# Row- and column-tiled attention with separate sums for all blocks, and a rearranged start, in a fused attention and gated feed-forward kernel

## The chip, the cores and the metric

The kernel runs on one core of one Trainium2 chip. The metric is the device time of one execution in microseconds (us). Runs of one kernel that lie more than 1.5% above its fastest are called slow and are left out of the ratios. The kernel before takes 248.42 us (median of three runs, 247.49 to 248.69).

## The reference, cut to what matters

```python
# q, k, v: (4, 8, 768, 64); mem_k, mem_v: (4, 8, 8, 64); fp32
for c in range(nc):                        # chunks of 32 tokens
    k_full = concat([mem_k, k[c_start-16 : c_end+8]])   # 8 memory rows, then a band of up to 56
    v_full = concat([mem_v, v[same rows]])
    scores = q_c @ k_full.T / sqrt(64)
    a = exp(scores - max); a = a / (sum(a) + 1e-9)
    out[c] = a @ v_full
x = out, as (3072 tokens, 512)
y = (relu(x @ w_gate) * (x @ w_val)) @ w_out          # 512 -> 1536 -> 512
```

## The kernel before: the parts that matter here

The kernel works on eight blocks of 384 tokens. Each block has attention for four pairs of heads, twelve feed-forward units (a gate product and a value product, 128 columns of the inner dimension each) and three output units. The attention of block n+1 is woven between the units of block n, so that the tensor engine (PE) always has something to do. A block's attention for one pair of heads is: scores on PE, an exponential on ACT, values and sums on PE, the reciprocal of the sums on ACT (a logarithm, then an exponential of its negative), and a multiply on DVE.

For blocks 2 to 7 the kernel before loads keys and queries as rows, turns them by a DMA transpose, and lets POOL spread the queries of two heads into a block-diagonal operand, so that one 128-row product gives the scores of both. A 128-column product gives the values (64 columns) and the sums (64 columns of ones, so the sum arrives 64 times) of one head at once:

```python
X = xps.tile([128, 2, 512], F32, name="x_ps")       # one PSUM tile of two banks, used by every pair of blocks 2 to 7

def turn_dma(n):                                    # SP queue: two DMA transposes
    nc.sync.dma_start_transpose(kT, k16s[n % 2]); nc.sync.dma_start_transpose(qTs[n], q16s[n])

def spread_q(n, eng):                               # POOL, 1.46 us each, two a block
    for hh in range(2):
        s = slice(D * hh, D * hh + D)
        eng(qbds[n % 2][s, :, :, hh, :]..., qTs[n][s]...)

def step_s(n, hp):                                  # scores of a pair of heads
    for i in range(NQ):
        nc.tensor.matmul(sc[...192 columns...], lhsT=kT[:, i, hp, :], rhs=qb[:, i, hp]..., start=True, stop=True)
    # ... three exponentials on ACT

def step_v(n, hp):                                  # values and sums together; bank hh holds head hh
    for i in range(NQ):
        for hh in range(2):
            nc.tensor.matmul(X[:, hh, QB * i:QB * i + QB], lhsT=vw[:, i, 2 * hp + hh, :],
                             rhs=ex[:, i, hh, :], start=True, stop=True)
    ln = rpool.tile([D, 2, TB], F32, name="ln")
    nc.scalar.activation(ln, X[D:128, :, 0:TB], ACT.Ln, scale=1.0 / 64.0)

def step_e(n, hp):                                  # reciprocal, to SBUF
    nc.scalar.activation(rinv, lns.pop((n, hp)), ACT.Exp, scale=-1.0, bias=mln64[0:D, :])

def step_m(n, hp):                                  # two multiplies on DVE
    for hh in range(2):
        nc.vector.tensor_tensor(out=xT[D * hh:D * hh + D, hp, :], in0=X[0:D, hh, 0:TB], in1=rinv[:, hh, :], op=ALU.mult)

# ... feed-forward: g and v in two one-bank tiles of a pool of four
units[n] = [(fps.tile([128, 512], F32, tag="f", name=nm)[:, 0:TB], w, m) for m in ms for w, nm in ((wg, "g_ps"), (wv, "v_ps"))]

# ... order of the first part: attention of block 0, one unit of block 0, attention of block 1 ...
loads(2); turn_dma(2); spread_q(2, pool_copy); loads(3)     # after all weights, the output weights wo included
for m in range(2, NDC):
    ffn_unit(0, m); ffn_unit(1, m)
# ... then the six output units of blocks 0 and 1, with block 2's attention between them
```

Blocks 0 and 1 use another path: keys and queries are turned by PE, and values and sums are already split into 64-column tiles.

The softmax here doesn't subtract the row's maximum and nothing guards it: scores larger than these inputs give would overflow.

## Time and profile before

| What | Where it is read | Value |
|---|---|---|
| span of the profiled execution | page, head | 247.0 us |
| PE busy | page, part 1 | 233.5 us, 95% |
| period of one block in steady state | chain, timeline | 26.05 us |
| longest wait of PE after the start | waits | 3.3 us, for POOL's spread of block 2's queries |

The first lines are from the page: the head, PE in part 1, and the rows of PE, its granted clock and the DMA engines over 40 slices of the span, in tenths.

```profile
span 247.0 us, 4433 instructions
...
PE 233.5 (95%) x1676; PEld 135.4 (55%) x1676; DVE 99.7 (40%) x180; ACT 141.5 (57%) x269; POOL 112.6 (46%) x143
...
PE   7998989999499979999999999999999999999993
...
PEclk9999999999779999999999999999999999999998
DMA  6989999999399749997992999199711200030012
```

PE is full nearly everywhere, and from the sixteenth slice on without a gap: the kernel is bound by PE. There is one deep dent, in slice 11 (a smaller one in slice 15), and the clock is low in slices 11 and 12. The timeline of PE shows that place (columns: start, duration, engine, line, operation, operands, and in brackets the idle time before it and who ended it):

```profile
61.13 0.81 PE L331 MATMUL v_ps<-xT,wv 128*128 128x384 f16 x4
65.28 0.80 PE L253 MATMUL sc_ps<-qbd,kT 128*128 128x192 f16 x4 [3.34 <-POOL qbd L226]
65.88 5.33 PE L354 MATMUL o_ps<-wo,gv 128*128 128x512 f16 x12
```

PE waits 3.34 us for block 2's queries. Then twelve output matmuls take 5.33 us. At full clock twelve take about 2.6 us (36 take 7.77), so the half clock (granted clock 0.50 from 65 to 70 us) costs another 2.7 us. The views of the stretches show that a steady block leaves no room at all (columns: stretch, its length, then busy time and count of each engine, the granted clock, the DMA share, GB/s):

```profile
107.82:133.87 26.05, 26.05 (x181) 15.60 (x180) 11.10 (x20) 17.78 (x36) 14.54 (x16) 1.00 1.34 137
```

PE is busy 26.05 of 26.05 us. ACT is busy 17.78 and DVE 11.10. Time taken off ACT or DVE buys nothing there, and time put on PE costs all of itself, 24 pairs of heads long.

### The profile page before, as it was taken

What the parts mean: (1) busy time and instruction counts of PE and PEld (TensorE: products, weight loads), DVE (VectorE), ACT (ScalarE), POOL (GpSimd) and SP (SyncE); (2) the same over time, 40 slices, a digit from 0 to 9 for tenths busy, and PEclk for the clock granted to TensorE, in tenths of its full rate; (3) what the DMA queues carried; (4) which work ended last, traced back from release to release, by engine and by line L of the source; (5) the groups of instructions that cost most, each with busy time, mean ns of one, the idle gap of its engine ahead of it and who ended that gap; (6) DMA issues with size and microseconds to landing.
All of it is one profiled execution on the core that took longest, in us unless ns stands there. A gap on an engine that the chain in (4) does not pass through costs nothing.

```text
span 247.0 us, 4433 instructions
## 1 busy us (share of the span) xinstructions
PE 233.5 (95%) x1676; PEld 135.4 (55%) x1676; DVE 99.7 (40%) x180; ACT 141.5 (57%) x269; POOL 112.6 (46%) x143
## 2 busy tenths in 40 slices
PE   7998989999499979999999999999999999999993
PEld 2564546666245446655665466646664566556641
DVE  7666544434002134560456136521662146404410
ACT  3473763333247947872878278836884488533321
POOL 8699649960992079419905950892040000000000
PEclk9999999999779999999999999999999999999998
DMA  6989999999399749997992999199711200030012
GB/s 173 186 112 158 195 205 194 191 150 186 22 145 185 164 125 120 128 123 116 180 158 62 122 202 175 18 153 189 137 23 45 85 1 3 2 125 0 3 42 85
DMA packets 114111, 28.95 MB, mean 117 GB/s; under 512 B 101834, under 2 KB 111018, under 8 KB 114090
## 3 DMA queue, kind: packets, MB, share of 16 engines
q0 software_dynamic: 84896, 14.74, 76.7%
q1 hardware_dynamic: 28362, 13.14, 23.2%
q10 hardware_dynamic: 832, 0.79, 1.3%
q8 instruction: 13, 0.21, 0.3%
q14 instruction: 8, 0.07, 0.1%
HBM read 31.16 MB, written 6.29 MB: 152 GB/s over the span
## 4 chain that ended last, share of the span: by engine, by line
PE 71%; POOL 9%; DMA 9%; issue 7%; ACT 2%; DVE 0%; SPq 0%; POOLq 0%
PE g_ps L331 23%; PE v_ps L331 23%; PE o_ps L354 19%; DMA kst<-in_k_dram 4%; PE x_ps L273 3%; PE sc_ps L253 3%; DMA vwin<-in_v_dram 3%; POOL vwin L128 2%; POOL qbd L226 2%; DMA qT<-q16n 2%; POOL k L128 1%; POOL q16n L149 1%; POOL lq L480 1%; POOL lk L479 1%; ACT lnw L308 1%
## 5 line engine op out<-in xcount | busy, mean ns | idle before, releaser
L339 DVE TENSOR_TENSOR gv<-v_ps,gr 128x384 f16<-128x384 f32 x96 | 53.4, 557 | 97.4 <-ACT gr L338 71.4
L331 PE MATMUL g_ps<-xT,wg 128*128 128x384 f16 x384 | 80.0, 326 | 1.6 <-DVE xT L315 1.6
L331 PE MATMUL v_ps<-xT,wv 128*128 128x384 f16 x384 | 80.0, 326 | 0.2 <-ACT o_sb L357 0.2
L354 PE MATMUL o_ps<-wo,gv 128*128 128x512 f16 x288 | 66.9, 390 | 0.0
L338 ACT ACTIVATE gr<-g_ps 128x384 f16<-128x384 f32 x96 | 46.7, 487 | 31.4 <-DVE gv L339 21.8
L331 PEld LDWEIGHTS <-wv 128*128 128x128 f16 x384 | 36.4, 98 | 24.7 <-issue 2.5
L331 PEld LDWEIGHTS <-wg 128*128 128x128 f16 x384 | 37.2, 98 | 23.1 <-issue 0.4
L354 PEld LDWEIGHTS <-gv 128*128 128x128 f16 x288 | 28.6, 100 | 33.3 <-issue 2.7
L226 POOL COPY qbd<-qT 64x1536 f16<-64x1536 f16 x12 | 17.5, 1462 | 60.8 <-DMA qT<-q16n 60.4
L288 DVE TENSOR_TENSOR xT<-x_ps,rinv 64x384 f16<-64x384 f32 x48 | 26.4, 550 | 26.0 <-ACT rinv L281 25.7
L357 ACT COPY o_sb<-o_ps 128x512 f32<-128x512 f32 x24 | 14.1, 587 | 37.7 <-PE o_ps L354 37.7
L260 ACT ACTIVATE ex<-sc_ps,bias 128x256 f16<-128x256 f32 x72 | 28.6, 467 | 7.4 <-PE sc_ps L253 7.4
L128 POOL DMA_DIRECT2D vwin<-in_v_dram x32 | 29.1, 941 | 0.8 <-PE v_ps L331 0.6
L276 ACT ACTIVATE ln<-x_ps 64x768 f32<-64x768 f32 x24 | 19.4, 807 | 13.5 <-PE x_ps L273 13.4
L281 ACT ACTIVATE rinv<-ln,mln 64x768 f32<-64x768 f32 x24 | 22.2, 924 | 0.1
L128 POOL DMA_DIRECT2D k<-in_k_dram x24 | 21.5, 905 | 0.0
L149 POOL DMA_DIRECT2D q16n<-in_q_dram x24 | 18.7, 805 | 0.0
L253 PE MATMUL sc_ps<-qbd,kT 128*128 128x192 f16 x96 | 12.1, 250 | 4.3 <-POOL qbd L226 4.3
L273 PEld LDWEIGHTS <-vwin 128*128 128x128 f16 x192 | 11.1, 99 | 5.3 <-issue 1.4
L273 PE MATMUL x_ps<-ex,vwin 128*128 128x96 f16 x192 | 12.3, 207 | 1.1 <-ACT ex L260 1.1
L253 PEld LDWEIGHTS <-kT 128*128 128x128 f16 x96 | 8.7, 99 | 7.8 <-issue 4.8
L431 PE MATMUL idle<-filler 128*128 128x512 f16 x28 | 10.0, 491 | 1.3 <-DVE filler L370 1.3
(70 smaller groups left out, 104.6 us busy)
## 6 DMA issues: line engine op xcount, KB each, us to landing
out_dram<-o_sb SPq DMA_DIRECT2D x24, 256.0 KB
vwin<-in_v_dram POOLq DMA_DIRECT2D x24, 120.0 KB, 6.3
q16n<-in_q_dram POOLq DMA_DIRECT2D x24, 96.0 KB, 4.9
k<-in_k_dram POOLq DMA_DIRECT2D x18, 120.0 KB, 4.3
wo<-in_moe_w_out_dram POOLq DMA_DIRECT2D x3, 512.0 KB, 13.6
wg<-in_moe_w_gate_dram POOLq DMA_DIRECT2D x2, 512.0 KB, 9.8
wv<-in_moe_w_val_dram POOLq DMA_DIRECT2D x2, 512.0 KB, 11.6
kst<-in_k_dram SPq DMA_DIRECT2D x4, 224.0 KB
```

The lines of the kernel that those rows point to most:

```text
L128: pool_dma(dsts[p][NMEM + m0:NMEM + m1, i, :, 0:D], src)
L149: pool_dma(q16s[n][:, i], src)
L226: eng(qbds[n % 2][s, :, :, hh, :].rearrange("p i a m -> p (i a) m"), qTs[n][s].rearrange("p i a m -> p (i a) m"))
L253: nc.tensor.matmul(sc[:, i // 2, 192 * (i % 2):192 * (i % 2) + 192], lhsT=kT[:, i, hp, :], rhs=qb[:, i, hp].rearrange("p h m -> p (h m)"), ...
L260: nc.scalar.activation(dst, src, ACT.Exp, scale=SCALE, bias=bias[:, g:g + 1])
L273: nc.tensor.matmul(X[:, hh, QB * i:QB * i + QB], lhsT=vw[:, i, 2 * hp + hh, :], rhs=ex[:, i, hh, :], start=True, stop=True)
L281: nc.scalar.activation(rinv, lns.pop((n, hp)), ACT.Exp, scale=-1.0, bias=mln64[0:D, :])
L288: nc.vector.tensor_tensor(out=xT[D * hh:D * hh + D, hp, :], in0=X[0:D, hh, 0:TB], in1=rinv[:, hh, :], op=ALU.mult)
L331: nc.tensor.matmul(ps, lhsT=w[:, f, 128 * m:128 * m + 128], rhs=xTs[n][:, f, :], start=(f == 0), stop=(f == NFC - 1))
L338: nc.scalar.activation(gr, g_ps, ACT.Relu)
L339: nc.vector.tensor_tensor(out=gvs[n][:, m, :], in0=v_ps, in1=gr, op=ALU.mult)
L354: nc.tensor.matmul(o_ps, lhsT=gvs[n][:, m, 128 * t:128 * t + 128], rhs=wo[:, m, :], start=(m == 0), stop=(m == NDC - 1))
```

## The change

The change gives all blocks one way of doing attention. Scores use two 64-row tiles, so that POOL's spread and its buffers go. Sums (`step_d`) are products of their own with a small tile of ones, apart from the values (`step_v`), both in 64-column tiles, so that the reciprocal is one wide operation for both heads (128x384), its logarithm in place in PSUM. The gate and value products of a unit share one two-bank PSUM tile. Block 0's units begin earlier and run while block 1's rows load; block 2's keys and queries load before the output weights. Heads 4 to 7 of block 0 are cast by the DMA that loads them.

```diff
-    rpool = ctx.enter_context(tc.tile_pool(name="rpool", bufs=2))
+    rpool = ctx.enter_context(tc.tile_pool(name="rpool", bufs=4))
-    fps = ctx.enter_context(tc.tile_pool(name="fps", bufs=4, space=bass.MemoryType.PSUM))
+    fps = ctx.enter_context(tc.tile_pool(name="fps", bufs=2, space=bass.MemoryType.PSUM))
     X = xps.tile([128, 2, 512], F32, name="x_ps")
+    xo, xs = X[:, 0, 0:TB], X[:, 1, 0:TB]
...
-    def spread_q(n, eng): ...
+    def score_mms(n, hp, sc, start):
+        for i in range(NQ):
+            for hh in range(2):
+                s = slice(D * hh, D * hh + D)
+                nc.tensor.matmul(sc[:, hh, QB * i:QB * i + QB], lhsT=kT[s, i, hp, :], rhs=qT[s, i, hp, :], ...)
...
+    def step_d(n, hp):
+        ...     nc.tensor.matmul(xs[D * hh:D * hh + D, QB * i0:QB * i1], lhsT=ones[:, kind, :], rhs=ex[:, hh, i0:i1, :], ...)
+    def step_l(n, hp):
+        nc.scalar.activation(xs, xs, ACT.Ln, scale=1.0 / 64.0)
+    def step_e(n, hp):
+        nc.scalar.activation(rinv, xs, ACT.Exp, scale=-1.0, bias=mln64)
     def step_v(n, hp):
+        ...     nc.tensor.matmul(xo[D * hh:D * hh + D, QB * i:QB * i + QB], lhsT=vw[:, i, 2 * hp + hh, :], rhs=ex[:, hh, i, :], ...)
+    def step_m(n, hp):
+        nc.vector.tensor_tensor(out=x_of(n)[:, hp, :], in0=xo, in1=rinvs.pop((n, hp)), op=ALU.mult)
...
+        units[n] = [(fps.tile([128, 2, 512], F32, tag="f", name="f_ps"), m) for m in ms]
...
+    loads_kq(2)
     for a in range(0, NDC, 4):
         pool_dma(wo[:, a:a + 4, :], wo_src[:, a:a + 4, :])
+    turn_dma(2)
...
+    def run(order, n, first, gap, wait, turn_at):
+        ...     unit(b, x, between(n, [(w, hp) for hp in now for w in "dlv"]))
+                pieces(n, [("e", hp) for hp in now])
+    run([(1, m) for m in range(6)] + [(0, NDC + t) for t in range(NT)] + [(1, m) for m in range(6, NDC + NT)],
+        2, 6, 2, 2, 9)
     for n in range(2, NB):
+        loads(n + 2)
+        run([(n, u) for u in range(NDC + NT)], n + 1, 0, 3, 2, 9)
```

The order "dlv" is: sums, logarithm, values, and after the unit the exponential.

## The prediction

> **What bounds it now.** TensorE: busy 95% of the 247.0 us span (page, part 1). From 93 us on it is gap-free. The chain and the timeline show one block of 384 tokens every 26.05 us (107.82 to 133.87): 24 half units of 0.65, outputs 7.77, attention 2.68 (four times scores 0.33 and values 0.33). FFN and outputs of eight blocks are a floor of 187 us; attention of blocks 2 to 7 is 16; the tail after the last output matmul 3.8. The other 40 us are the target:
> - to 34.48 us (timeline, PE) the attention of blocks 0 and 1 stands nearly alone: only three FFN units (3.9 us) are done by then, so about 30.6 us of overhead;
> - at 61.8 the PE idles 3.4 us for block 2 (waits: scores <- POOL spread of q <- DMA transpose); the clock falls to half (PEclk 7 in two slices; twelve output matmuls at 427 ns), about 2.6 us more;
> - about 2 us of waits for block 3's spread and exponentials at 84 to 93.
>
> **What the change does.**
> 1. Scores and values are split into 64-row and 64-column tiles; no spread copy on POOL (1.46 us each, 12). This costs PE time: at 14 to 18 us of the trace, where such tiles already run, a pair of 96-column matmuls starts every 0.042 us, but each change of tile mode leaves a hole of 0.09 to 0.10 us. [...] Scores become 0.37 (two holes), sums and values together 0.56, so 0.93 against 0.66 per head pair: +0.27, times 24 = +6.4 us on the bottleneck.
> 2. ACT per head pair falls from about 2.9 to 2.3 us, DVE from 1.10 to 0.56. Both are off the path in steady state: worth nothing there. Pairing g and v in one PSUM tile frees them later (slack about 0.4 us by my sum): no stall expected, save about 1 us in block 2's denser schedule.
> 3. Start: block 0's FFN begins before block 1's attention, whose chains hide between units. My sum of the chain (cast, turn, copy about 1.1, scores, exp 0.81, ln 0.49, exp 0.61, multiply 0.56; one sum bank makes ln and exp serial) ends the first two units near 22 us: overhead about 19. Block 1 adds turns 3.6, scores and values 3.7, waits 2 to 3. So 30.6 becomes about 29.
> 4. Block 2's keys and queries load before the output weights and its scores come at about 55 us, when I expect the transposes done (about 51): saves the 3.4, 2.6 and most of 2 us. Loads then read about 0.39 MB/us (1.05 MB weight loads landing 2.6 us apart): weights for units 4 to 7 land about 24, block 1's rows 29, just in time.
>
> **Sum.** 187 + 22.3 + 19 + 9.5 + 1 + 3.8 = about 242.5 us of span; with 1.4 between span and time, 244. Range 240 to 248.5. Chances: faster by over 2% 0.40, within 2% 0.55, slower 0.05.
>
> **Right if** the block period is about 27.1 us with no PE idle in it; no idle over 3 us and no half clock after 25 us; the last FFN unit of block 0 and block 1's attention end by 43 to 46 us; POOL has no long wait for transposes. **Wrong if** mode holes hide behind preloaded weights (faster by up to 5 us); units of block 0 wait for weights, or block 2's transposes slip past 55 us (PE idle, half clock: 3 to 6 us slower); [...] or ACT delays stall the two PSUM pairs each unit.

## The result, and the profile after

The kernel after takes 275.06 us (median of four runs, 273.41 to 276.59), beside 248.56 of the kernel before (four runs). The ratio is 1.1075 (95% interval 1.0989 to 1.1161): 11% slower. Ratios in this document are the mean time of one kernel's fast runs over that of the other's fast runs of the same rounds, so not quite the ratio of the medians quoted. The profiled span grew from 247.0 to 274.6 us, where the prediction's sum was 242.5: 32.1 us were missed. The same lines of the page after:

```profile
span 274.6 us, 4565 instructions
...
PE 242.1 (88%) x1845; PEld 128.9 (47%) x1845; DVE 81.1 (30%) x161; ACT 128.5 (47%) x276; POOL 87.7 (32%) x116
...
PE   5957983889998999999899999899999998999994
...
PEclk9988999669999999999999999999999999999999
```

ACT, DVE and POOL have less to do, as intended, and yet PE now idles 32.5 us (274.6 less 242.1) where it idled 13.5. The list of PE's waits says for whom (columns: who waits for whom, us in total, times, longest):

```profile
PE x_ps L269 <- ACT x_ps L258: 13.6, 24, 0.6
PE x_ps L269 <- ACT rinv L262: 10.7, 7, 2.1
PE kq_ps L185 <- DMA rk<-in_mem_k_dram: 1.5, 1, 1.5
```

Line 269 is the value product, line 258 the logarithm of the sums, line 262 the exponential after it. The values need neither: they need the exponentials of the scores and the rows of v. And yet they wait for the reciprocal 31 times, together 24.3 us. Two pieces of the timeline show one pair of heads of block 3, first on PE, then on ACT:

```profile
105.59 0.36 PE L254 MATMUL x_ps<-ex,ones 128*64 128x288 f16 x4
106.52 0.36 PE L269 MATMUL x_ps<-ex,vwin 128*64 128x96 f16 x8 [0.57 <-ACT x_ps L258]
106.81 0.82 PE L286 MATMUL f_ps<-xT,wv 128*128 128x384 f16 x4
```

```profile
105.99 0.47 ACT L258 ACTIVATE x_ps<-x_ps 128x384 f32<-128x384 f32 x1 [0.45 <-PE x_ps L254]
```

The sums end at 105.95, the logarithm runs from 105.99 to 106.46, and only then do the values start. From the first sum to the next feed-forward matmul, 1.22 us pass. The chain of work that ended last gives the period of a block (start, duration):

```profile
88.66 7.77 PE o_ps L311 x36
...
118.84 7.77 PE o_ps L311 x36
...
149.03 7.77 PE o_ps L311 x36
```

A block takes 30.19 us (149.03 less 118.84), in place of 26.05 before and of the 27.1 predicted. In block 1 it is worse, because there the order is sums, logarithm, exponential, values, with no unit between; the timeline of PE at 41 to 53 us:

```profile
41.10 0.36 PE L254 MATMUL x_ps<-ex,ones 128*64 128x288 f16 x4
43.56 0.36 PE L269 MATMUL x_ps<-ex,vwin 128*64 128x96 f16 x8 [2.10 <-ACT rinv L262]
43.85 0.82 PE L286 MATMUL f_ps<-xT,wg 128*128 128x384 f16 x4
...
47.99 0.36 PE L269 MATMUL x_ps<-ex,vwin 128*64 128x96 f16 x8 [2.10 <-ACT rinv L262]
...
51.59 0.53 PE L269 MATMUL x_ps<-ex,vwin 128*64 128x96 f16 x8 [1.19 <-ACT rinv L262]
52.05 1.46 PE L286 MATMUL f_ps<-xT,wg 128*128 128x384 f16 x4
```

Each pair idles PE up to 2.10 us, and from about 49 us on four matmuls take 1.46 us in place of 0.82: the clock is at half until 59.4 us (granted clock 0.52 from 49.0 to 59.4 us). The same happened at 18.8 to about 22 us (0.50). Block 1's attention ends at 57 us; 43 to 46 was predicted.

### The profile page after: what moved, and what is told of

Its sections match the earlier page's. It is cut to its first block, busy times and chain, and to the rows that moved or that the text cites. A ratio compares the mean times of both kernels' runs of the same rounds, so it can differ in the third digit from the quotient of the medians.

```text
span 274.6 us, 4565 instructions
## 1 busy us (share of the span) xinstructions
PE 242.1 (88%) x1845; PEld 128.9 (47%) x1845; DVE 81.1 (30%) x161; ACT 128.5 (47%) x276; POOL 87.7 (32%) x116
## 4 chain that ended last, share of the span: by engine, by line
PE 85%; ACT 9%; DMA 2%; issue 1%; DVE 1%; DVEq 0%; ACTq 0%; POOLq 0%
PE f_ps L286 49%; PE o_ps L311 23%; ACT x_ps L258 5%; PE x_ps L269 4%; PE x_ps L254 3%; PE sc_ps L218 3%; DMA rk<-in_mem_k_dram 2%; ACT rinv L262 1%; ACT ex L240 1%; PE kq_ps L185 1%; PE kq_ps L190 1%; ACT gr L292 1%; DVE gv L293 0%; DVE kq L199 0%; PE sc_ps L226 0%
## 5 line engine op out<-in xcount | busy, mean ns | idle before, releaser
L293 DVE TENSOR_TENSOR gv<-f_ps,gr 128x384 f16<-128x384 f32 x96 | 53.4, 557 | 151.6 <-ACT gr L292 151.6
L286 PE MATMUL f_ps<-xT,wg 128*128 128x384 f16 x384 | 81.5, 333 | 0.8 <-DVE gv L293 0.8
L286 PE MATMUL f_ps<-xT,wv 128*128 128x384 f16 x384 | 81.6, 333 | 0.0
L292 ACT ACTIVATE gr<-f_ps 128x384 f16<-128x384 f32 x96 | 47.0, 491 | 71.4 <-PE f_ps L286 69.4
L269 PE MATMUL x_ps<-ex,vwin 128*64 128x96 f16 x256 | 12.1, 215 | 24.3 <-ACT x_ps L258 13.6
L269 PEld LDWEIGHTS <-vwin 128*64 128x64 f16 x256 | 11.0, 113 | 29.4 <-issue 29.0
L273 DVE TENSOR_TENSOR xT<-x_ps,rinv 128x384 f16<-128x384 f32 x32 | 17.8, 555 | 23.3 <-PE x_ps L269 13.8
L258 ACT ACTIVATE x_ps<-x_ps 128x384 f32<-128x384 f32 x32 | 15.3, 478 | 15.6 <-PE x_ps L254 15.5
L262 ACT ACTIVATE rinv<-x_ps,mln 128x384 f32<-128x384 f32 x32 | 18.4, 576 | 0.2
L254 PE MATMUL x_ps<-ex,ones 128*64 128x96 f16 (+1 forms) x128 | 11.7, 264 | 0.0
```

The lines of the kernel that those rows point to most:

```text
L254: nc.tensor.matmul(xs[D * hh:D * hh + D, QB * i0:QB * i1], lhsT=ones[:, kind, :], rhs=ex[:, hh, i0:i1, :], start=True, stop=True)
L258: nc.scalar.activation(xs, xs, ACT.Ln, scale=1.0 / 64.0)
L262: nc.scalar.activation(rinv, xs, ACT.Exp, scale=-1.0, bias=mln64)
L269: nc.tensor.matmul(xo[D * hh:D * hh + D, QB * i:QB * i + QB], lhsT=vw[:, i, 2 * hp + hh, :], rhs=ex[:, hh, i, :], start=True, stop=True)
L273: nc.vector.tensor_tensor(out=x_of(n)[:, hp, :], in0=xo, in1=rinvs.pop((n, hp)), op=ALU.mult)
L286: nc.tensor.matmul(ps[:, a, 0:TB], lhsT=(wg, wv)[a][:, f, 128 * m:128 * m + 128], rhs=xTs[n][:, f, :], start=(f == 0), stop=(f == NFC - 1))
```

## The experiments

**Theory A.** The two banks of `X` are one tile to the program, so every access to it waits for the last access of it by another engine, whichever half that touched: values wait for the logarithm, and the logarithm for the multiply of the pair before. **Rival B.** The pairing of gate and value products in one two-bank tile, two deep in place of four one-bank tiles, starves PE. **Rival C.** It is the hardware: PE and ACT, or row and column tiles, get in each other's way in PSUM, so the wait is for the banks and not for the order of the program. **Rival D.** The rearranged start and the transposes are what cost. The first four runs tell these apart. They ran on one chip, with seven runs of the kernel before (median 248.95).

### Run 1: sums and values as two tiles

```diff
-    X = xps.tile([128, 2, 512], F32, name="x_ps")
-    xo, xs = X[:, 0, 0:TB], X[:, 1, 0:TB]
+    xo, xs = (xps.tile([128, 512], F32, name=nm)[:, 0:TB] for nm in ("xo_ps", "xs_ps"))
```

> The changed kernel with the value output and the sums in two PSUM tiles of one bank each in place of two halves of one two-bank tile; nothing else. Theory A (the built program makes every access of the shared tile wait for the last one, so the value matmuls wait for the logarithm, or for logarithm and exponential, of the sums): the 24.3 us of TensorE waits on x_ps vanish, the block period falls from 30.2 to about 27.1 us, the half clock at 50 to 59 us vanishes, and the time falls from 275 to 244 to 250 us. Theory B (the time is tile-mode holes and the paired g and v tile): it changes by less than 4 us.

Measured: 255.04 us, 1.0225 times the kernel before (1.0162 to 1.0289). About 20 us of the loss (275.06 less 255.04) come back by a declaration. The same place in this run's timeline of PE:

```profile
106.65 0.36 PE L253 MATMUL xs_ps<-ex,ones 128*64 128x288 f16 x4
106.84 0.34 PE L268 MATMUL xo_ps<-ex,vwin 128*64 128x96 f16 x8
107.11 0.82 PE L285 MATMUL f_ps<-xT,wv 128*128 128x384 f16 x4
```

Values follow sums without an idle time, and from the first sum to the next feed-forward matmul it is 0.46 us in place of 1.22. The difference, 0.76 us, is the idle 0.57 and the overlap of two groups of matmuls that the wait had cut apart. Four pairs make 3.04 us a block, and the block period is indeed 27.15 us in place of 30.19. Here PE writes one bank while ACT works in place in the other, and the output is correct. They are the same two banks: in the built programs (each instruction with the semaphores that it waits for) the tile `X` of the kernel after lies in PSUM banks 2 and 3, and the two tiles of this run lie there too. The same products in the same order and the same banks lose their wait when nothing but the declaration changes, so rival C falls.

The time is over the 244 to 250 us that were expected: PE now waits 5.3 us for the transposed queries of block 2, of which run 3 tells more.

### Run 2: gate and value products as two tiles, sums and values still one

```diff
-    fps = ...(name="fps", bufs=2, ...)
+    fps = ...(name="fps", bufs=4, ...)
-        units[n] = [(fps.tile([128, 2, 512], F32, tag="f", name="f_ps"), m) for m in ms]
+        units[n] = [([fps.tile([128, 512], F32, tag="f", name=nm) for nm in ("g_ps", "v_ps")], m) for m in ms]
```

(The tiles of turned keys and queries were split likewise.)

> The changed kernel with g and v (and the turned k and q) in separate one-bank PSUM tiles, four buffers, as before the change; the sums still share a tile with the values. Theory A: relu starts about 0.65 us earlier in each unit, but the waits on x_ps stay: 271 to 275 us, block period still about 30 us. Theory B: most of the loss comes back, under 260 us.

Measured: 274.36 us, ratio 1.1024 (1.0939 to 1.1109). The waits of PE are what they were after the change:

```profile
PE x_ps L271 <- ACT x_ps L260: 13.6, 24, 0.6
PE x_ps L271 <- ACT rinv L264: 10.3, 7, 2.0
```

Rival B falls. After the change, the relu of a unit does wait for both halves of the shared tile, for the same reason as in theory A, but that wait is ACT's, and PE hardly felt it (0.8 us, once, in the kernel after's list of waits).

### Run 3: both split

> Both splits. Theory A: what the prediction assumed, so 242 to 247 us, block period about 27.1 us (26.05 before, plus 0.27 for each of four head pairs), no TensorE wait over 2 us after 26 us. Theory B: about as the g and v split alone.

Measured: 253.81 us, ratio 1.0202 (1.0132 to 1.0273), span 251.3. The edit is that of runs 1 and 2 together. Two lines of its chain give the period:

```profile
107.89 7.77 PE o_ps L312 x36
...
135.04 7.77 PE o_ps L312 x36
```

This is 27.15 us, where 27.1 was predicted. The first two units of block 0 are done at 21.0 us (22 predicted), and block 1's attention at 44.7 (43 to 46 predicted). With the unexpected wait gone the prediction's terms can be read one by one, and one stands out as wrong; it is why this run missed the 242 to 247 us expected of it. The timeline of PE:

```profile
52.06 2.75 PE L312 MATMUL o_ps<-wo,gv 128*128 128x512 f16 x12
61.21 0.51 PE L219 MATMUL sc_ps<-qT,kT 64*128 64x96 f16 x8 [6.40 <-DMA qT<-q16n]
61.65 6.60 PE L312 MATMUL o_ps<-wo,gv 128*128 128x512 f16 x18
```

Block 2's scores wait 6.40 us for the transpose of the queries, and then eighteen output matmuls take 6.60 us where they take 4.06 at full clock (the same view of the kernel after); the row of the granted clock shows 7 and 6 tenths in the two slices from 56.5 to 69.1 us. That is 8.9 us, and the prediction's 242.5 and 8.9 make 251.4, against a span of 251.3. (The other terms can still be off in ways that cancel.) The DMA view of 40 to 63 us tells why the transposes were late (columns: target, source, queue, kind, times, median us from issue to landing):

```profile
kT<-k SPq DMA_TRANSPOSE x1, 13.2
qT<-q16n SPq DMA_TRANSPOSE x1, 11.1
```

Both were in flight together with the output weights and block 2's and 3's rows, the DMA engines full throughout (9 in all 40 slices of that view). The keys landed at 56.2 us and the queries at 61.1. SP issues one after the other, and issuing the keys' transpose took 6.8 us here, so that the queries' was not issued before 50.0 us. So part of rival D stands, as a second cause beside A.

### Run 4: one shared tile, but the values recorded ahead of the logarithm

```diff
-                unit(b, x, between(n, [(w, hp) for hp in now for w in "dlv"]))
+                unit(b, x, between(n, [(w, hp) for hp in now for w in "dvl"]))
```

(Block 1's four pairs likewise; block 0 is as after the change.)

> The changed kernel with one shared tile, but the value matmuls recorded ahead of the logarithm in blocks 1 to 7, so that they follow the sums at once. Theory A: the waits of the values on the logarithm go, though the logarithm now waits for the values and for the multiply of the pair before: block period 27.1 to 27.5 us, time 246 to 254 us. If the loss were a conflict of the hardware on the two banks rather than the order of waits, the period would stay near 30 us.

Measured: 253.06 us (median of the three fast runs; the fourth, 255.72, is slow), ratio 1.0153 (1.0068 to 1.0238), period 27.15 us, both as theory A expected. The tile is the same and the banks are the same; only the order differs. What remains of the waits of line 269 is block 0:

```profile
PE x_ps L269 <- ACT rinv L262: 4.1, 3, 1.5
```

Theory A stands. (This run alone would not have ruled out rival C: with the values first, they no longer meet the logarithm in time. Run 1 does.) It could have been read before any run. In the built program of the kernel after, 31 of the 32 value products carry a wait for ACT's semaphore on their first matmul; in run 1 none does, in run 4 three do. Such a row reads:

```
756 L269 Matmult x_ps<-ex,vwin_101 64x96 [waits Activation_49]
```

### Runs 5 and 6: block 2's scores later; the transposes shielded

The second cause was looked into from run 3 on. Run 5 moves block 2's scores behind the first output unit, after all twelve feed-forward units of block 1, and block 3's scores two units later; where a pair falls into an output unit, its exponential is put inside that unit too. Run 6 is run 5 with two tiny copies on POOL that read the turned keys and queries, put ahead of the loads of the output weights, so that nothing after them is issued until the transposes have landed. Runs 5 to 8 ran on one chip, with seven runs of the kernel before (median 248.76).

```diff
# run 5, against run 3
-    run([(1, m) for m in range(6)] + [(0, NDC + t) for t in range(NT)] + [(1, m) for m in range(6, NDC + NT)], 2, 6, 2, 2, 9)
+    run([(1, m) for m in range(NDC)] + [(b, NDC + t) for b in range(2) for t in range(NT)], 2, 12, 1, 1, 14)
-        run([(n, u) for u in range(NDC + NT)], n + 1, 0, 3, 2, 9)
+        run([(n, u) for u in range(NDC + NT)], n + 1, 2 if n == 2 else 0, 3, 2, 9)
# ... and "dlev" in place of "dlv" in output units
# run 6, against run 5
+    turn_dma(2)
+    gate = const.tile([1, 2], F16, name="gate")
+    nc.gpsimd.tensor_copy(gate[:, 0:1], kTs[2][0:1, 0, 0, 0:1])
+    nc.gpsimd.tensor_copy(gate[:, 1:2], qTs[2][0:1, 0, 0, 0:1])
     for a in range(0, NDC, 4): pool_dma(wo...)
-    turn_dma(2)
```

> Both splits, and the scores of block 2 put after the first output unit that follows all twelve FFN units of block 1 (as late as before the change), with block 3's scores two units later. Theory C (what is left over the prediction after the splits is one wait of 6.4 us for the transpose of block 2's queries, and the half clock it causes): the wait and the half clock go, 242 to 246 us. Rival D (the leftover is tile-mode holes and the FFN order): no gain, still 252 to 255 us.

> The same, and a tiny POOL copy of the transposed tiles holds back the output weights and all later loads until block 2's transposes have landed. Theory E (the transposes were slow, 13 and 11 us from issue to landing, because output weights and later loads shared the DMA engines): keys land within about 5 us of issue and queries by about 53 us in place of 61. The time is then about that of the ungated one, or some us worse if the weights come late. If they are slow by themselves, they land near 60 us again.

Measured: run 5 251.34 us, ratio 1.009 (1.0041 to 1.014); run 6 253.66, ratio 1.0195 (1.0147 to 1.0243). Run 5 missed the 242 to 246 us expected of it; run 6 did what was expected of its transposes, and cost some us, which its expectation had allowed. Run 5 has no wait for block 2 any more; the wait sits at block 3, whose transposes were moved late as well and again share the DMA engines (the queries' took 10.5 us from issue to landing, at 78.26 to 88.77 us, and the row of DMA stands at 9 there):

```profile
PE sc_ps L219 <- DMA qT<-q16n: 3.6, 1, 3.6
```

Run 6 shows how long the same two transposes take when they are left alone, in the same view as in run 3:

```profile
kT<-k SPq DMA_TRANSPOSE x1, 4.5
qT<-q16n SPq DMA_TRANSPOSE x1, 4.4
```

The queries landed at 49.9 us in place of 61.1. So the load of other transfers makes the transposes 13.2 and 11.1 us; by themselves they take 4.5 and 4.4. But what was held back comes later: PE waits 0.5 us for the output weights, and block 3's wait is 4.1 us. The shield moves the wait.

### Run 7: run 5 with one 128-column product for values and sums in blocks 2 to 7

This takes back the one part of the change that the prediction had put at +0.23 us of PE a pair (0.56 in place of 0.33), and keeps the row-tiled scores.

```diff
     def step_d(n, hp):
+        if n >= 2:
+            for i in range(NQ):
+                for hh in range(2):
+                    nc.tensor.matmul((xo, xs)[hh][:, QB * i:QB * i + QB], lhsT=vwins[n % 2][:, i, 2 * hp + hh, :],
+                                     rhs=ex[:, hh, i, :], start=True, stop=True)
+            return
# ... logarithm, exponential and two multiplies as in the kernel before; vwin with columns of ones
```

> The late version, with blocks 2 to 7 taking values and sums by one 128-column product (ones beside the values), as before the change, so without the two 64-column tile groups; scores stay in row tiles. Theory A plus the prediction's costing (sums and values in column tiles 0.56 us, this 0.33): 0.23 less for each of 24 head pairs, period 27.15 to about 26.25 us, time 5 to 6 us under the late version, 236 to 241 us, unless ScalarE (about 97% busy in the FFN part by my sum) holds it. If tile modes cost nothing: no difference.

Measured: 245.56 us (243.90 to 247.09), ratio 0.9858 (0.9797 to 0.9919). Two lines of the chain give the period:

```profile
154.49 7.77 PE o_ps L339 x36
...
180.75 7.77 PE o_ps L339 x36
```

It is 26.26 us in place of 27.15: 0.22 us a pair, as predicted. Six blocks make 5.3 us of it, and run 5 and run 7 of the same chip differ by 5.8. (The absolute range of the expectation, 236 to 241 us, was missed because run 5 itself was slower than hoped.) In this profiled run no wait for a transpose was left either. (The expectation's 97% for ACT was the author's estimate. Measured: in the feed-forward part of a block of the kernel before, 115.60 to 133.87 us, ACT is busy 15.11 of 18.27 us; in run 7 it is busy 18.33 of 26.05 us from 107.82 to 133.87 us.)

### Run 8: the kernel before with row-tiled scores and no spread

```diff
-            nc.tensor.matmul(sc[...192...], lhsT=kT[:, i, hp, :], rhs=qb[:, i, hp]..., ...)
+            for hh in range(2):
+                s = slice(D * hh, D * hh + D)
+                nc.tensor.matmul(sc[:, hh, QB * i:QB * i + QB], lhsT=kT[s, i, hp, :], rhs=qT[s, i, hp, :], ...)
-    spread_q(2, pool_copy)      # and at blocks 3 to 7
```

> The kernel before with only the scores of blocks 2 to 7 in two row tiles, so no spread copy on POOL. By the prediction's costing: 0.04 us per head pair is added (about 1 us), the two waits for the spread (4.3 us) shrink to the transposes' own, and part of the half clock may go: 242 to 247 us against 248.5. If row tiles were what slowed the changed kernel, it would be slower than before.

Measured: 249.88 us, ratio 1.0031 (0.9981 to 1.0082): the same, where a gain was expected. The wait for POOL's spread is gone, and a longer one for the transposed queries has taken its place:

```profile
66.41 0.51 PE L254 MATMUL sc_ps<-qT,kT 64*128 64x96 f16 x8 [4.66 <-DMA qT<-q16n]
```

In the kernel before the queries had landed by 62.26 us, when the spread starts, 0.3 us after PE ran out of work; the spread itself made the other 3.0 us of the wait. Here they landed 4 us later, though their transpose was issued earlier (56.57 us, against 57.46). What differs is POOL (its timeline before, then in this run):

```profile
62.26 2.98 POOL L226 COPY qbd<-qT 64x1536 f16<-64x1536 f16 x2 [8.02 <-DMA qT<-q16n]
65.17 3.53 POOL L128 DMA_DIRECT2D k<-in_k_dram  x4
```

```profile
54.03 3.52 POOL L127 DMA_DIRECT2D k<-in_k_dram  x4
```

Before, POOL stood in front of the spread for 8.02 us and issued block 3's loads only after it; without the spread it issues them from 54.03 us on, and the transposes share the DMA engines with them: the queries' took 9.79 us from issue to landing, in place of 4.74. The spread had been a shield like the two copies of run 6. This is read from the two traces; no run tests it alone.

The period is 26.27 us: row-tiled scores cost 0.05 us a pair, near the 0.04 predicted (0.37 less 0.33).

### Run 9: the kernel before with block 2's keys and queries loaded ahead of the output weights

```diff
+    load_band(2, k, k16s); load_k_mem(2); load_q_tokens(2); turn_dma(2); spread_q(2, pool_copy)
     for a in range(0, NDC, 4):
         pool_dma(wo[:, a:a + 4, :], wo_src[:, a:a + 4, :])
...
-    loads(2); turn_dma(2); spread_q(2, pool_copy)
+    load_band(2, v, vwins); load_v_mem(2)
```

> The kernel before, with block 2's keys and queries loaded ahead of the output weights, and the spread copies of block 2 (which wait for the transposes) left on POOL ahead of the weights' issue, so that the transposes share the DMA engines with nothing large. Nothing else of the change. Theory E: both transposes land near 50 us, the wait of 3.4 us at 61.8 and the half clock behind it (2.6 us) go, 241 to 245 us against 248.5. If transposes are slow by themselves, or the wait only moves to block 3, it stays within 2 us of before.

Measured: 249.83 us, ratio 1.0026 (0.9984 to 1.0069), with eleven runs of the kernel before on that chip (median 248.69). Again a gain was expected and none came. The transposes had landed by 52.7 us, when POOL's spread of the queries starts, and what had been ahead of them was now late:

```profile
PE x_ps L273 <- DMA vwin<-in_v_dram: 1.7, 3, 0.6
PE o_ps L354 <- DMA wo<-in_moe_w_out_dram: 1.7, 1, 1.7
```

The clock fell here as well (7 tenths in the twelfth slice, 68.1 to 74.3 us). In the row of DMA in the page before, nine of the first ten slices stand at 8 or 9: the loads of the first 60 us are all needed, and putting one ahead puts another behind. This is where, as far as these runs show, the promise of the prediction's step 4 went.

### Runs 10 to 12: looking for a version that beats both

Run 10 is run 7 with the values and later loads of every block held behind its transposes, as in run 6, and with the last pair of block 1 inside the last unit of block 0. Run 11 is run 7 with block 3's transposes one output unit earlier, six output buffers in place of three, and the same place for the last pair. Run 12 is run 11 with more filler matmuls before the first work of PE.

```diff
# run 10, against run 7
-        loads(n + 2)
+        if n + 1 < NB:
+            hold(n + 1); loads_v(n + 1)        # hold: POOL copies one element of kT and of qT
+        if n + 2 < NB:
+            loads_kq(n + 2)
# ... (cut: block 2's hold and transposes ahead of the output weights; block 1's last pair as in run 11)
# run 11, against run 7
-    opool = ...(name="opool", bufs=3)
+    opool = ...(name="opool", bufs=6)
-        2, 12, 1, 1, 14)
+        2, 12, 1, 1, 13)
-    ffn_unit(0, 11); step_d(1, 3); step_l(1, 3); step_e(1, 3); step_v(1, 3); step_m(1, 3)
+    ffn_unit(0, 11, [lambda w=w: w(1, 3) for w in (step_d, step_l, step_e, step_v, step_m)])
# run 12, against run 11
-    fill(9)
+    fill(12)
```

> The late version with 128-column values (a_xf_late_wide), and in each block the values' loads and the loads of the block after are held behind that block's transposes; the last pair of block 1 is put inside the last unit of block 0. Theory E: no TensorE wait for a transpose in any block, no half clock after 25 us, 238 to 243 us, and less spread between runs than 243.9 to 247.1. If holding loads back makes values or output weights late, there is a new wait on vwin or wo and no gain over 245.6.

> The late version with 128-column values, nothing held back; block 3's transposes issued one output unit earlier, six output tiles in place of three so that the later stores do not stop ScalarE, and the last pair of block 1 put inside the last unit of block 0. Expected if the spread of a_xf_late_wide (243.9 to 247.1 us) is a wait for block 3's transposes in some runs: 241 to 244.5 us in all runs, over 2% faster than before. If the spread is something else: 244 to 247 us as it was.

> The tuned version with 12 filler matmuls in place of 9 at the start; TensorE waits there for the keys' memory rows until 6.9 us anyway, so they cost nothing. If gaps of TensorE in the first 20 us let its clock fall to half at 18 to 24 us (seen in the trace of the tuned version and of the changed kernel): 0.5 to 2 us better, 242.5 to 244.5 us, over 2% faster than before. If the half clock there does not depend on the filler: no change.

Run 10 measured 258.07 us, ratio 1.0356 (1.032 to 1.0393). It was a mistake: in later blocks there was nothing to shield, and the values came late instead, each time.

```profile
PE xo_ps L257 <- DMA vwin<-memv: 8.9, 13, 3.3
```

Run 11 measured 244.54 us (243.79 to 245.64), ratio 0.9823 (0.9789 to 0.9858); 244.5 at most was expected of every run, and three of six were above it. Its profile has no wait for a transpose, but half clock in its fourth slice (feed-forward matmuls 0.32 us apart in place of 0.16), after an idle time of 1.67 us. (Its first turn of keys, at 7.01 us, takes 1.06 us too, where run 12 takes 0.63, though the row of the clock shows nothing there; why stays open.) Run 12 measured 242.54 us (242.27 to 243.57), ratio 0.9783 (0.9745 to 0.9822), on another chip, near the low end of what was expected. The row of the granted clock in run 11 and in run 12:

```profile
PEclk9997999999999999999999999999999999999999
```

```profile
PEclk9999999999999999999999999999999999999999
```

Run 12 beats both kernels. It is 2.2% under the kernel before, with an interval of 1.8 to 2.5%, so that "faster by over 2%" is likely but not certain. The filler of run 12 runs where PE waited 1.73 us for a load in run 11, so it costs no time of its own. That it keeps the clock up is what the two rows suggest (7 and 9 tenths in the fourth slice; mean granted clock of the two profiled runs 0.992 and 1.000); the intervals of the two ratios overlap, and no run of both on one chip was made, so the size of the filler's gain stays open. The same holds for the gain of run 11 over run 7.

## Why the prediction was wrong

**Step 2 failed.** It said: "Both are off the path in steady state: worth nothing there. Pairing g and v in one PSUM tile frees them later [...]: no stall expected". For the gate and value pair it asked when the tile comes free, found a slack of 0.4 us, and was right (run 2). For sums and values, the other pair of halves in one tile, it looked only at how busy ACT and DVE are. It speaks of "one sum bank" as if the halves were independent, and in the built program they are not: the value product waits for the logarithm of the sums, because both touch `X`. That put ACT on PE's path once for 31 of the 32 pairs of heads. The 32.1 us that were missed are nearly all of this:

| Term | How it is read | us |
|---|---|---|
| 24 pairs of blocks 2 to 7 | 24 times 0.76 (1.22 after, 0.46 in run 1) | 18.2 |
| 7 waits in blocks 0 and 1 | waits, for the exponential of the reciprocal | 10.7 |
| half clock at 18.8 to 22 and 49 to 59.4 us | estimate: 8 feed-forward matmuls 0.32 us apart in place of 0.16, and four groups of four in 1.46 to 1.49 us in place of 0.82 | about 4 |

The sum is about 33. Run 1 gives back less, 23.1 us of the span (274.6 less 251.5), because PE then comes to block 2's scores before their transposes have landed, and a loss appears that the kernel after had hidden: 5.3 us of wait and 2.3 of half clock (18 output matmuls in 6.39 us, not 4.06) in run 1 (step 4). Splitting the tile (run 1) or changing the order (run 4) takes it away, and splitting the other pair (run 2) does not.

**Step 1 was right.** The profile after could not show it, since the period was 30.19 us. With the tile split the period is 27.15, where 27.1 was predicted, and runs 7 and 8 confirm its two parts: 0.22 for values and sums, 0.05 for scores. The holes of 0.09 to 0.10 us that the prediction read at changes of tile mode are in the trace before: from one group of eight 96-column matmuls to the next it is 0.28 us where the mode changes (14.86 to 15.14) and 0.19 where it does not (15.14 to 15.33). Why a change leaves a hole is not shown.

**Step 3 was right once the wait is gone:** 21.0 us for the first two units and 44.7 for block 1's attention in run 3, against 22 and 43 to 46.

**Step 4 was wrong, and the kernel after hid it.** It expected the transposes of block 2 done at about 51 us. In the kernel after the queries landed at 63.3 us by the trace, but its PE was so late that nothing waited for them. In run 3 they landed at 61.1, and cost 8.9 us, 6.4 of wait and 2.5 of half clock. The prediction had named this risk at 3 to 6 us. The term was mis-sized: 51 us fits transposes without load, 4.5 and 4.4 us when shielded (run 6), and not the 13.2 and 11.1 that they took among the weight loads (run 3). Dropping the spread, which step 1 counted as work saved, also took away what had held POOL's later loads back (run 8). Runs 8 and 9 show that neither dropping the spread nor loading earlier would have helped the kernel before by itself.

So even without the surprise the change would have lost: by run 3, 2.0%. It puts 6.6 us on the bottleneck (24 times 0.275, from 27.15 and 26.05), to unload engines that were not one.

## What to carry to other kernels

Two halves of one tile are one thing to the program that orders the engines: before a change that puts an in-place operation of another engine on one half, read in the built program's waits what the other half's next access waits for, or give each half its own tile, which costs nothing here (the same two banks, and a block of 27.15 us in place of 30.19). Busy shares cannot show a wait that does not exist yet; costing a change needs the order of accesses to each shared buffer too. A transfer's duration must be taken from a stretch as loaded as the one in which it will run (4.5 us held apart and 13.2 us under load here). And work off the critical path can hold back the loads behind it: before it is removed, ask what its engine will issue earlier.

## What these runs show of the hardware

- A change of tile mode left holes of 0.09 to 0.10 us (the kernel before, 14.8 to 16.9 us). Row-tiled scores cost 0.05 us a pair of heads (run 8), separate column-tiled sums and values 0.22 (run 7 against run 5).
- In the kernel after, the clock fell at about 49 us with no idle time over 2.10 us: two idle times of 2.10 us began at about 41.5 and 45.9 us, with work between them. It then stayed at half to 59.4 us (granted clock 0.52) with idle times of 1.19 us. In run 11 it fell after an idle time of 1.67 us, and in run 12 it did not after one of 1.8 us in the same place. Why it fell in one and not in the other, these runs do not show.
- Runs 1 and 3: two engines worked in two PSUM banks at once (output correct; sums, then values in 0.46 us without a wait). In the kernel after, the waits of the built program were for a whole tile of two banks, and cost 0.76 us a pair.
- The 0.52 MB of turned keys (128 x 2048 fp16) took 4.5 us from issue to landing with the other loads held back (run 6), which is 116 GB/s with the start of the transfer in it, and 13.2 us among weight loads (run 3), 40 GB/s. While the two transposes alone moved (45 to 49 us of run 6), the row of the DMA view stands at 185 to 217 GB/s.
